# A slot's entry in DRAM widened from 4 to 64 bytes, with the lists read two jobs ahead, in a router of an attention and mixture-of-experts kernel

## The chip, the cores and the metric

The kernel runs on one core of one Trainium2 chip. The metric is the device time in microseconds (us); lower is better.

## The reference

Three stages follow each other; all data are float32 at the edges.

```python
# 1. linear attention with decay: batch 4, heads 8, sequence 768, head size 48
for t in range(S):
    cur = einsum('bhd,bhe->bhde', u[None] * kt, vt)
    y[:, :, t] = einsum('bhd,bhde->bhe', rt, state + cur)
    state = w[None, :, :, None] * state + einsum('bhd,bhe->bhde', kt, vt)
# 2. x has N = 3072 rows of D = 384; 8 experts, F = 1024; each row goes to one expert
logits = x @ w_gate
expert_idx = argmax(logits, axis=1)
for e in range(E):
    mask = expert_idx == e
    h = maximum(x[mask] @ w1[e], 0.0)
    out[mask] = gate_w[mask, None] * (h @ w2[e])
# 3. one dense layer for all rows, 384 -> 2048 -> 384, with an ELU between
h = x @ w_in
return where(h > 0, h, exp(minimum(h, 0)) - 1) @ w_out
```

## The kernel before, in words

**Attention and routing.** The sequence is cut into six chunks of 128 steps; a chunk has 4 x 128 tokens. While a chunk's attention runs on all engines, the chunk before it is routed. For each batch index of a chunk, `slots` works out where each of 128 tokens belongs: expert times 512 plus its rank among that expert's tokens so far, so that tokens of one expert get consecutive slots. `store` writes the tokens' rows to the DRAM array `xl` with one SP transfer for each chunk, and `place` writes, for each of the four batch indices, the token's row number into its slot of the DRAM array `xi`: one scatter (an indirect transfer issued by POOL, helper `scatter`, line 98) of 128 entries. There are 24 scatters. At the start `blank` fills `xi` and a second DRAM array, `idl`, with the number of an empty row (lines 274 and 275).

**The jobs.** The first expert layer runs as nine jobs (`JOBS`, called u = 0 to 8): two halves of the fullest expert, then the other seven experts by size. The order is worked out on the chip; SP and ScalarE read it into registers (`TENSOR_LOAD`). For each job, `load_i` has SP read the job's list of row numbers from `xi` (line 758; it must wait until all scatters so far have landed), `load_x` has POOL gather the rows from `xl` by that list (line 770; `xe` for jobs 0 to 2, `xg` later), `note` has SP write the list on to `idl` (line 783), `turn` transposes the rows on TensorE (line 798), and `layer1` and `layer2_columns` multiply (lines 829 and 869). Job 0 starts before routing is done, on the first four chunks' tokens, and overlaps the last chunk.

**Weights.** `Stream` reads weights in chunks of 768 KB through two buffers `raw` (line 695, on SP's queue) and splits each into a rounded half (ScalarE, line 705) and the rest (VectorE, line 711). Chunks 0 to 3 belong to jobs 0 and 1, chunks 4 to 7 to job 2, and so on. Each product is made of three matmuls, so both halves are needed. In job 0, activations are split the same way (ScalarE line 837, VectorE line 848).

**Order.** All steps up to the end of job 1's transposes are listed by `put(...)` and then called in the order of the table `ORDER`, written out by number; each engine runs its share in that order. The jobs from 1 on are a plain loop in `experts`, in which loads and splits are called between the matmuls.

**The second layer** goes through all 3,072 rows in six blocks of 512 (`layer2_rows`, line 1023). Its output rows are scattered to the output tensor (24 scatters of 128 rows, line 98 again) at positions that `tokens` works out from `idl`: the list is read as 24 rows of 128 (line 994), copied, transposed on TensorE (line 999) and turned into row numbers by a few small VectorE instructions.

Of the kernel before, what the change touches and what calls it, by code (L numbers as in the profile page):

```python
# [7 lines left out]
F32 = mybir.dt.float32  # L8
F32R = mybir.dt.float32r
BF16 = mybir.dt.bfloat16  # L10
I32 = mybir.dt.int32
# [4 lines left out]
PSUM = bass.MemoryType.PSUM  # L16

B, H, S, D = 4, 8, 768, 48
N, DM, E, F1, F2 = 3072, 384, 8, 1024, 2048
C = 128  # L20
NC_ = S // C
NP = H // 2
CAP = 512
HALF = CAP // 2
WIDTH = (480, 456, 424, 416, 408, 392, 384, 376)
JOBS = [(0, 0, HALF), (0, HALF, WIDTH[0] - HALF)] + [(p, 0, WIDTH[p]) for p in range(1, E)]
NJ = len(JOBS)
# [3 lines left out]
BLANK = N  # L31
# [34 lines left out]
)  # L66


# [35 lines left out]
def attention(tc, g, ctx, rkT, kv, wT, uT, wg):  # L104
    nc = tc.nc
# [123 lines left out]
    ef = con.tile([128, E], F32, name="ef")  # L229
    it = con.tile([128, ITEMS], I32, name="it")  # L230
    tid_i = con.tile([128, NC_, B], I32, name="tid_i")
    pos = con.tile([128, NC_, B], I32, name="pos")
    none = con.tile([128, (N + CAP) // 128], I32, name="none")
    zi = con.tile([128, E * CAP // 128], I32, name="zi")
    kr = con.tile([128, B, DM], F32, name="kr")
    acc, ones = g.acc, g.ones
    box = {}
# [15 lines left out]
    def iotas():  # L253
        nc.gpsimd.iota(ei, pattern=[[1, E]], base=0, channel_multiplier=0)
        nc.gpsimd.iota(it, pattern=[[1, ITEMS]], base=0, channel_multiplier=0)
        nc.gpsimd.tensor_copy(out=g.item, in_=it)
        for p in range(E):
            nc.gpsimd.memset(g.width[:, p:p + 1], float(WIDTH[p]))
        nc.gpsimd.iota(pos, pattern=[[B * C, NC_], [1, B]], base=0, channel_multiplier=B)
        nc.gpsimd.iota(tid_i, pattern=[[C, NC_], [S, B]], base=0, channel_multiplier=1)  # L260

    def router_constants():
# [3 lines left out]

    def blank():

        z = early_x.tile([128, 2, DM], F32, tag="xe", name="blank")[:, 0]
        nc.gpsimd.memset(z, 0.0)  # L270
        nc.gpsimd.memset(none, BLANK)
        nc.gpsimd.memset(zi, BLANK)
        nc.sync.dma_start(out=g.xl[BLANK:BLANK + 1], in_=z[0:1])
        nc.sync.dma_start(out=g.idl.rearrange("(p n) o -> p (n o)", p=128), in_=none)
        nc.sync.dma_start(out=g.xi.rearrange("(p n) o -> p (n o)", p=128), in_=zi)

    def krow(c, b):
        then(nc.vector.tensor_tensor(out=kr[:, b], in0=k_b[:, c % 2, b], in1=pkr.rearrange("s p h d -> s (p h d)"),
# [201 lines left out]
    def place(c):  # L480

        for b in range(B):
            scatter(tc, nc, g.apart, "slots", out=g.xi,
                    out_offset=bass.IndirectOffsetOnAxis(ap=r_t[c].si[:, b:b + 1], axis=0),
                    in_=pos[:, c, b:b + 1], in_offset=None, bounds_check=CAP * E - 1, oob_is_err=False)

    def counts():

# [101 lines left out]
    jobs.x_tile = lambda u, shape: (early_x if u < 2 else jobs.keep).tile(  # L590
        shape, F32, tag="xe", name="xe")
    jobs.xT_tile = lambda u, shape: (wk if u == 0 else jobs.keep).tile(shape, F32R, tag="kr", name="xTe", bufs=1)
    jobs.ix_tile = lambda shape: jobs.keep.tile(shape, I32, tag="ix", name="ix", bufs=NJ)
    jobs.h_tile = lambda f, shape: wk.tile(shape, F32R, tag="rp", name="he", bufs=4)

    def first_rows():
# [4 lines left out]
        put(jobs.note, 0)  # L601

    def next_rows():
        for u in range(1, NJ):
            put(jobs.load_i, u)
        for u in (1, 2):
            put(jobs.load_x, u)
        put(jobs.note, 1)
# [115 lines left out]
class Jobs:  # L724
# [27 lines left out]
    def load_i(self, u):  # L752

        p, at, n = JOBS[u]
        j = 2 if n <= HALF else 4
        ix = self.ix[u] = self.ix_tile([n // j, j])
        src = self.g.xi.rearrange("(e s) o -> e s o", e=E)[self.g.stream.which(p), at:at + n]
        self.nc.sync.dma_start(out=ix.unsqueeze(2), in_=src.rearrange("e (p j) o -> p (e j) o", j=j))

    def behind(self, ins):  # L760

# [1 line left out]

    def load_x(self, u, chunks=NC_):
        ix = self.ix[u]
        r, j = ix.shape
        x = self.x[u] = self.x_tile(u, [r, j, DM])
        rows = B * C * chunks if chunks < NC_ else BLANK + 1
        for i in range(j):
            ins = self.nc.gpsimd.indirect_dma_start(  # L770
                out=x[:, i, :], out_offset=None, in_=self.g.xl[0:rows],
                in_offset=bass.IndirectOffsetOnAxis(ap=ix[:, i:i + 1], axis=0), bounds_check=rows - 1,
                oob_is_err=False)
            if u > 2:
                self.behind(ins)

    def note(self, u):

        nc, g, (p, at, n) = self.nc, self.g, JOBS[u]
        if p > 0:  # L780
            at = nc.sync.value_load(g.lead[0:1, p:p + 1], min_val=0, max_val=sum(WIDTH[0:p]))
        ix = self.ix[u]
        nc.sync.dma_start(out=g.idl[bass.ds(at, n)].rearrange("(p j) o -> p j o", j=ix.shape[1]),
                          in_=ix.unsqueeze(2))

    def turn(self, u, k):
        self.turn_mm(u, k)
# [96 lines left out]
def experts(tc, g, ctx, wpk2, out):  # L884
# [77 lines left out]
    plan = overflow_plan(nc, g, own.enter_context(tc.tile_pool(name="m_p", bufs=1)), g.p_m)  # L962
    for u in range(1, NJ):
        for f in range(8):
            if 1 < u < NJ - 1 and f == 1:
                jobs.load_x(u + 1)
            stream.ahead(min(jobs.chunk(u, f) + 3, 4 * E + 4) if u > 1 else 4 + max(0, f // 2 - 1))
            if u + 1 < NJ and 5 <= f:
                jobs.turn(u + 1, f - 5)
                if f == 7:  # L970
                    jobs.note(u + 1)
            if f < 4 or u == 2:
                next(clearing, None)
            next(plan, None)
            for _ in range(1 + (f % 4 < 3 if u > 1 else f in (2, 4, 6))):
                next(narrowing, None)
            jobs.step(u, f)
# [7 lines left out]
    wq = own.enter_context(tc.tile_pool(name="n_w", bufs=4))  # L985
    ap = own.enter_context(tc.tile_pool(name="n_a", bufs=1, space=PSUM))
    lp = own.enter_context(tc.tile_pool(name="n_l", bufs=3, space=PSUM))
    tp_ps = own.enter_context(tc.tile_pool(name="n_t", bufs=1, space=PSUM))
    stream.pool = lambda i: wq if i >= 4 * E + 4 else stream.wc
    jobs.l_tile = lambda n: lp.tile([128, n], F32, tag="l", name="psl")  # L990
    t = jobs.keep.tile([128, 256 + 5 * N // 128], F32, tag="xe", name="idT")
    idi, idT = t[0:N // 128, 0:128].bitcast(I32), t[0:N // 128, 128:256]
    ids = t[:, 256:].bitcast(I32).rearrange("q (k n) -> q k n", k=5)
    nc.sync.dma_start(out=idi, in_=g.idl[0:N].rearrange("(n p) o -> n (p o)", p=128))

    def tokens():

        ps = tp_ps.tile([128, N // 128], F32, name="psi")
        nc.tensor.transpose(ps, idT, g.ident[0:N // 128, 0:N // 128])
        at, row, chunk, seq, none = (ids[:, k] for k in range(5))  # L1000
        nc.vector.tensor_copy(out=row, in_=ps)
        nc.vector.tensor_scalar(out=chunk, in0=row, scalar1=9, scalar2=7, op0=ALU.logical_shift_right,
                                op1=ALU.logical_shift_left)
        nc.vector.tensor_scalar(out=at, in0=row, scalar1=2, scalar2=127, op0=ALU.logical_shift_right,
                                op1=ALU.bitwise_and)
        nc.vector.tensor_scalar(out=seq, in0=row, scalar1=3, scalar2=None, op0=ALU.bitwise_and)
        nc.vector.tensor_scalar(out=none, in0=row, scalar1=float(BLANK), scalar2=OOB, op0=ALU.is_ge, op1=ALU.mult)
        nc.vector.tensor_tensor(out=at, in0=at, in1=chunk, op=ALU.add)
        nc.vector.tensor_tensor(out=at, in0=at, in1=none, op=ALU.add)
        nc.vector.scalar_tensor_tensor(out=at, in0=seq, scalar=float(S), in1=at, op0=ALU.mult, op1=ALU.add)  # L1010
# [27 lines left out]
    for u in range(NJ, NJ + 6):  # L1038
        for f in range(16):
            if u == NJ:  # L1040
                stream.ahead(jobs.chunk(u, f) + 3)
            if u == NJ and f == 2:
                nc.vector.tensor_copy(out=idT, in_=idi)
            if u == NJ and f == 4:
                tokens()
            if u + 1 < NJ + 6 and f in (6, 8, 10):
                jobs.take(u + 1, f // 2 - 3)
            if u == NJ + 5 and f == 14:
                jobs.LAG = 3
            jobs.step(u, f)  # L1050
# [142 lines left out]
def tile_kernel(tc, rkT, kv, wT, uT, wg, wpk, wpk2, out):  # L1193
# [1 line left out]
    g = K()  # L1195
    g.tc = tc
    g.xl = tc.dram_tile([BLANK + 1, DM], F32, name="xl")
    g.xi = tc.dram_tile([E * CAP, 1], I32, name="xi")
    g.idl = tc.dram_tile([N + CAP, 1], I32, name="idl")
    g.w2f = wpk2 if wpk2.dtype == F32 else tc.dram_tile([1, 8, 128, 1536], F32, name="w2f")  # L1200
    with ExitStack() as ctx:
        pool = ctx.enter_context(tc.tile_pool(name="const", bufs=1))
# [83 lines left out]
```

## Time and profile before

| | |
|---|---|
| Median of 3 runs | 819.2 us (818.52 to 819.9) |
| The profiled execution | 810.9 us, of which 809.1 us are the span from the first to the last instruction |
| Granted TensorE clock, mean over the span | 0.975 |
| TensorE busy (matmuls) | 769.8 us, 95% |
| VectorE / ScalarE / POOL busy | 486.2 / 346.8 / 132.8 us |
| Data moved by DMA | 84.92 MB in 24,660 packets, 8,620 of them under 512 bytes |

The profile is of one execution; every duration below is of that one. Times in the timeline count from the span's start. A row of the timeline has its start, its duration, the engine, the line, what is written and read, and in brackets how long the engine had been idle before it and what ended that. PE is TensorE's matmuls, PEld its weight loads, DVE VectorE, ACT ScalarE, POOL GpSimd, SPq the issue of transfers by SyncE. "DMA to landing" is the time from a transfer's issue until its semaphore showed that it had arrived. The DMA share is the mean busy share of the core's 16 DMA engines. A granted clock of 1.00 is 2.4 GHz, 0.50 is 1.2 GHz.

### The profile page before, as it was taken

What the parts mean: (1) busy time and instruction counts of PE and PEld (TensorE: products, weight loads), DVE (VectorE), ACT (ScalarE), POOL (GpSimd) and SP (SyncE); (2) the same over time, 40 slices, a digit from 0 to 9 for tenths busy, and PEclk for the clock granted to TensorE, in tenths of its full rate; (3) what the DMA queues carried; (4) which work ended last, traced back from release to release, by engine and by line L of the source; (5) the groups of instructions that cost most, each with busy time, mean ns of one, the idle gap of its engine ahead of it and who ended that gap; (6) DMA issues with size and microseconds to landing.
All of it is one profiled execution on the core that took longest, in us unless ns stands there. A gap on an engine that the chain in (4) does not pass through costs nothing. (4 is left out here: it accounts for less than half of the span.)

```text
span 809.1 us, 13146 instructions
## 1 busy us (share of the span) xinstructions
PE 769.8 (95%) x5113; PEld 690.6 (85%) x5114; DVE 486.2 (60%) x905; ACT 346.8 (43%) x675; POOL 132.8 (16%) x191
## 2 busy tenths in 40 slices
PE   6798799849999999999999999999999999999996
PEld 4576677649999999999989999999999999999996
DVE  6895975525987888866577444444444534544443
ACT  3686676426644444444444333233333333333231
POOL 4343442512320221030000020020002002002002
PEclk9699899979999999999999999999999999999999
DMA  9889434956978777865231010010001001001001
GB/s 341 201 177 150 120 80 80 158 76 183 308 212 275 253 266 230 258 168 163 92 118 40 1 40 0 2 40 1 0 1 40 1 1 40 1 1 40 1 0 42
DMA packets 24660, 84.92 MB, mean 105 GB/s; under 512 B 8620, under 2 KB 9013, under 8 KB 24017
## 3 DMA queue, kind: packets, MB, share of 16 engines
q1 hardware_dynamic: 17776, 74.01, 33.7%
q0 software_dynamic: 6528, 9.89, 4.0%
q8 instruction: 42, 0.69, 0.4%
q14 instruction: 26, 0.20, 0.1%
q10 hardware_dynamic: 288, 0.13, 0.1%
HBM read 68.20 MB, written 15.79 MB: 104 GB/s over the span
## 5 line engine op out<-in xcount | busy, mean ns | idle before, releaser
L829 PE MATMUL psl<-xT,wc 128*128 128x512 f32 (+7 forms) x1368 | 319.7, 378 | 0.1
L829 PEld LDWEIGHTS psl<-xT,wc 128*128 128x128 f32 x1368 | 251.6, 188 | 31.9 <-DVE xT L815 0.9
L1023 PE MATMUL acc<-wc,h 128*128 128x384 f32 x1152 | 217.8, 337 | 0.1
L1023 PEld LDWEIGHTS acc<-wc,h 128*128 128x128 f32 x1152 | 204.6, 188 | 8.7 <-DVE h L851 0.4
L841 DVE TENSOR_SCALAR ex<-ex 128x512 f32<-128x512 f32 x96 | 40.9, 426 | 125.1 <-ACT ex L840 125.1
L840 ACT ACTIVATE ex<-psl 128x512 f32<-128x512 f32 x96 | 57.3, 597 | 134.9 <-PE psl L829 134.9
L843 ACT CAST h<-ex 128x512 fp32r<-128x512 f32 x96 | 59.6, 621 | 126.1 <-DVE ex L842 126.1
L869 PE MATMUL acc<-h,wc 128*128 128x224 f32 (+7 forms) x576 | 111.8, 339 | 0.0
L851 DVE TENSOR_TENSOR h<-ex,h 128x512 fp32r<-128x512 f32 x96 | 66.5, 692 | 65.9 <-ACT h L843 65.9
L711 DVE TENSOR_TENSOR wc<-raw,wc 128x768 fp32r<-128x768 f32 x80 | 73.1, 955 | 52.4 <-ACT wc L705 52.4
L869 PEld LDWEIGHTS acc<-h,wc 128*128 128x128 f32 x576 | 100.8, 188 | 1.9
L98 POOL DMA_INDIRECT out_dram<-y,idT x24 | 24.6, 1024 | 424.4 <-ACT y L1031 418.9
L705 ACT CAST wc<-raw 128x1536 fp32r<-128x1536 f32 x40 | 59.1, 1477 | 39.9 <-PE acc L869 27.2
L842 DVE TENSOR_TENSOR ex<-ex,psl 128x512 f32<-128x512 f32 x96 | 66.0, 688 | 3.3
L333 ACT ACTIVATE a<-ident,cs 128x128 f32<-128x128 f32 x192 | 59.1, 392 | 1.3 <-issue 1.2
L837 ACT ACTIVATE h<-psl 128x224 fp32r<-128x224 f32 (+7 forms) x64 | 31.5, 492 | 58.6 <-PE psl L829 56.0
L770 POOL DMA_INDIRECT xg<-xl,ix x24 | 34.5, 1437 | 131.5 <-PE psl L829 126.0
L349 DVE COPY_PREDICATED a<-above,psc 128x512 f32<-128x512 uint32 x48 | 33.3, 729 | 12.6 <-PE psc L341 10.6
L848 DVE SCALAR_TENSOR_TENSOR h<-psl,h 128x224 fp32r<-128x224 f32 (+7 forms) x64 | 35.3, 551 | 8.2 <-ACT h L837 8.2
L369 PE MATMUL pso<-a,v 128*48 128x128 f32 x384 | 28.1, 289 | 6.7 <-DVE a L349 6.2
L218 POOL TENSOR_TENSOR rt<-rkb,ex 128x512 f32<-128x512 f32 x20 | 24.0, 1208 | 61.7 <-DVE a L349 21.3
L341 PE MATMUL psc<-rt,kt 64*128 64x128 f32 x384 | 30.8, 300 | 1.6 <-DVE a L349 1.6
(179 smaller groups left out, 611.1 us busy)
## 6 DMA issues: line engine op xcount, KB each, us to landing
raw<-in_wpk_dram SPq DMA_DIRECT2D x32, 768.0 KB, 6.6
r<-in_wpk_dram SPq DMA_DIRECT2D x16, 768.0 KB, 5.8
w2f<-f SPq DMA_DIRECT2D x16, 384.0 KB, 5.3
raw<-w2f SPq DMA_DIRECT2D x8, 768.0 KB, 4.2
v<-in_kv_dram SPq DMA_DIRECT2D x6, 768.0 KB, 4.2
rkb<-in_rkT_dram SPq DMA_DIRECT2D x12, 384.0 KB, 7.6
xl<-x SPq DMA_DIRECT2D x6, 768.0 KB
kb<-in_kv_dram SPq DMA_DIRECT2D x5, 768.0 KB, 6.1
```

Source lines behind the costliest of these rows:

```text
L333: nc.scalar.activation(out=a[:, b, :], in_=g.ident, func=ACTF.Copy, scale=cs_t[c][:, b, p, hf:hf + 1])
L705: self.nc.scalar.copy(out=w[:, 0], in_=self.loaded[i])
L711: self.nc.vector.tensor_tensor(out=w[:, 1, at], in0=r[:, at], in1=w[:, 0, at].bitcast(F32), op=ALU.subtract)
L829: self.mm = nc.tensor.matmul(ps, self.w1(i, a, k, fi), xT[:, b, k], start=(m == 0), stop=(m == 8))
L840: nc.scalar.activation(out=ex, in_=ps, func=ACTF.Exp)
L841: nc.vector.tensor_scalar(out=ex, in0=ex, scalar1=1.0, scalar2=-1.0, op0=ALU.min, op1=ALU.add)
L842: nc.vector.tensor_tensor(out=ex, in0=ex, in1=ps, op=ALU.max)
L843: nc.scalar.copy(out=h[:, 0], in_=ex)
L848: nc.vector.scalar_tensor_tensor(out=h[:, 1], in0=ps, scalar=0.0, in1=h[:, 0].bitcast(F32), op0=ALU.max, op1=ALU.subtract)
L851: nc.vector.tensor_tensor(out=h[:, 1], in0=self.ex, in1=h[:, 0].bitcast(F32), op=ALU.subtract)
L869: nc.tensor.matmul(self.acc[u][k], w[:, a, 128 * k:128 * k + 128], h[:, b], start=(f == 0 and m == 0), stop=(f == 7 and m == 2))
L1023: nc.tensor.matmul(acc, h[:, a, 128 * j:128 * j + 128], jobs.w2(i, b, fi), start=(f == 0 and m == 0), stop=(f == 15 and m == 2))
```

## The change

Every entry of `xi` and of `idl` becomes a row of `COPIES` = 16 equal 32-bit numbers, 64 bytes. The scatters write 16 numbers for each token (`pos` holds each row number 16 times); the lists are read and noted whole, and the gathers take the first of each 16. `blank` fills the wider arrays from one tile, with a source row that is used twice. Of the later jobs' lists, which were all read in one go after the last scatter, only those of jobs 1 and 2 are read there; the loop over the jobs reads the list of job u + 2 at the beginning of job u, and five list buffers take turns where each job had its own. In the second layer the list is read straight into 128 partitions, so the copies and the transpose go, and the VectorE instructions come four steps later. `ORDER` is renumbered for the list reads that left it.

```diff
+COPIES = 16
...
-    pos = con.tile([128, NC_, B], I32, name="pos")
-    none = con.tile([128, (N + CAP) // 128], I32, name="none")
-    zi = con.tile([128, E * CAP // 128], I32, name="zi")
+    pos = con.tile([128, NC_, B, COPIES], I32, name="pos")
...
-        nc.gpsimd.iota(pos, pattern=[[B * C, NC_], [1, B]], base=0, channel_multiplier=B)
+        nc.gpsimd.iota(pos, pattern=[[B * C, NC_], [1, B], [0, COPIES]], base=0, channel_multiplier=B)
...
-        z = early_x.tile([128, 2, DM], F32, tag="xe", name="blank")[:, 0]
+        z = early_x.tile([128, 2, DM], F32, tag="xe", name="blank")
+        z, none = z[:, 0], z[:, 1].bitcast(I32)
         nc.gpsimd.memset(z, 0.0)
         nc.gpsimd.memset(none, BLANK)
-        nc.gpsimd.memset(zi, BLANK)
         nc.sync.dma_start(out=g.xl[BLANK:BLANK + 1], in_=z[0:1])
-        nc.sync.dma_start(out=g.idl.rearrange("(p n) o -> p (n o)", p=128), in_=none)
-        nc.sync.dma_start(out=g.xi.rearrange("(p n) o -> p (n o)", p=128), in_=zi)
+        for t in (g.idl, g.xi):
+            n = t.shape[0] // 256 * COPIES
+            nc.sync.dma_start(out=t.rearrange("(p k n) o -> p k (n o)", p=128, k=2),
+                              in_=none[:, 0:n].unsqueeze(1).to_broadcast([128, 2, n]))
...
-                    in_=pos[:, c, b:b + 1], in_offset=None, bounds_check=CAP * E - 1, oob_is_err=False)
+                    in_=pos[:, c, b], in_offset=None, bounds_check=CAP * E - 1, oob_is_err=False)
...
-    jobs.ix_tile = lambda shape: jobs.keep.tile(shape, I32, tag="ix", name="ix", bufs=NJ)
+    jobs.ix_tile = lambda shape: jobs.keep.tile(shape, I32, tag="ix", name="ix", bufs=5)
...
-        for u in range(1, NJ):
+        for u in (1, 2):
             put(jobs.load_i, u)
...
-        ix = self.ix[u] = self.ix_tile([n // j, j])
+        ix = self.ix[u] = self.ix_tile([n // j, j, COPIES])
...
-                in_offset=bass.IndirectOffsetOnAxis(ap=ix[:, i:i + 1], axis=0), bounds_check=rows - 1,
+                in_offset=bass.IndirectOffsetOnAxis(ap=ix[:, i, 0:1], axis=0), bounds_check=rows - 1,
...
     for u in range(1, NJ):
         for f in range(8):
+            if u + 2 < NJ and f == 0:
+                jobs.load_i(u + 2)
...
-    idi, idT = t[0:N // 128, 0:128].bitcast(I32), t[0:N // 128, 128:256]
-    nc.sync.dma_start(out=idi, in_=g.idl[0:N].rearrange("(n p) o -> n (p o)", p=128))
+    rows = t[:, 0:COPIES * N // 128].rearrange("q (n o) -> q n o", o=COPIES)
+    nc.sync.dma_start(out=rows, in_=g.idl[0:N].rearrange("(n p) o -> p n o", p=128))
...
-        ps = tp_ps.tile([128, N // 128], F32, name="psi")
-        nc.tensor.transpose(ps, idT, g.ident[0:N // 128, 0:N // 128])
-        nc.vector.tensor_copy(out=row, in_=ps)
+        row = rows[:, :, 0]
...
-            if u == NJ and f == 2:
-                nc.vector.tensor_copy(out=idT, in_=idi)
-            if u == NJ and f == 4:
+            if u == NJ and f == 8:
                 tokens()
...
-    g.xi = tc.dram_tile([E * CAP, 1], I32, name="xi")
-    g.idl = tc.dram_tile([N + CAP, 1], I32, name="idl")
+    g.xi = tc.dram_tile([E * CAP, COPIES], I32, name="xi")
+    g.idl = tc.dram_tile([N + CAP, COPIES], I32, name="idl")
```

On SP, where weight chunk 3 has been issued and the lists of the later jobs are read, this stood before (partitions x elements behind each transfer; 104x4 is job 4's list, 112x2 job 1's, 96x4 job 7's):

```order
L695 DMA raw<-in_wpk_dram 128x1536
L688 TENSOR_LOAD order
L688 ISA x2
L758 ISA
L758 DMA ix<-xi 104x4
L758 ISA
L758 DMA ix<-xi 112x2
L688 TENSOR_LOAD order
L688 ISA x2
L758 ISA
L758 DMA ix<-xi 96x4
```

and this stands there now (112x32 is job 1's list, 114x64 job 2's, 106x64 job 3's; the other lines' numbers are two higher than before):

```order
L697 DMA raw<-in_wpk_dram 128x1536
L760 ISA
L760 DMA ix<-xi 112x32
L690 TENSOR_LOAD order
L690 ISA x2
L760 ISA
L760 DMA ix<-xi 114x64
L785 DMA idl<-ix 112x32
L690 TENSOR_LOAD order
L690 ISA x2
L760 ISA
L760 DMA ix<-xi 106x64
```

Before, five more lists, job 2's the sixth of the eight behind job 4's and job 1's, and then job 1's note stood ahead of the load of chunk 4; now that load comes right behind job 3's list, and job 1's note stands ahead of job 3's list.

At SP's start, the fills of the two arrays stand between the loads of k, v and r rows. Before:

```order
L143 DMA kb<-in_kv_dram 128x1536
L273 DMA xl<-blank 1x384
L274 DMA idl<-none 128x28
L275 DMA xi<-zi 128x32
L147 DMA v<-in_kv_dram 128x1536
```

Now:

```order
L145 DMA kb<-in_kv_dram 128x1536
L273 DMA xl<-blank 1x384
L276 DMA idl<-blank 256x1x224
L276 DMA xi<-blank 256x1x256
L149 DMA v<-in_kv_dram 128x1536
```

Nothing moved there; the two fills grew sixteenfold, in the same place of the queue.

## Rows read from the trace of the kernel before

**Rows 1.** The page's 40 slices: TensorE's busy tenths; GB/s moved by DMA

```profile
PE   6798799849999999999999999999999999999996
...
GB/s 341 201 177 150 120 80 80 158 76 183 308 212 275 253 266 230 258 168 163 92 118 40 1 40 0 2 40 1 0 1 40 1 1 40 1 1 40 1 0 42
```

**Rows 2.** Waits of PE: who waited for whom, us in total, times, longest

```profile
PE psl L829 <- DVE he L848: 11.0, 1, 11.0
PE pso L369 <- DVE a L349: 6.2, 1, 6.2
...
PE psq L798 <- DMA xe<-xl,ix: 0.9, 2, 0.5
```

**Rows 3.** Timeline, PE and ACT, 156 to 184 us

```profile
156.91 3.83 PE L829 MATMUL psl<-xTe,wc 128*128 128x256 f32 x27
...
168.68 1.47 ACT L705 CAST wc<-raw 128x1536 fp32r<-128x1536 f32 x1 [11.23 <-DMA raw<-in_wpk_dram]
...
172.82 2.26 PE L829 MATMUL psl<-xTe,wc 128*128 128x256 f32 x9 [11.02 <-DVE he L848]
...
183.43 0.55 PE L798 MATMUL psq<-ident,xe 112*128 112x112 f32 x4
```

**Rows 4.** Timeline, issues on SP, 141 to 182 us

```profile
141.10 0.34 SPq L783 DMA_DIRECT2D idl<-ix  x1
...
149.00 0.34 SPq L695 DMA_DIRECT2D raw<-in_wpk_dram  x1
...
172.56 8.60 SPq L758 DMA_DIRECT2D ix<-xi  x8
```

**Rows 5.** DMA issues of the whole span: count, KB each, median us to landing

```profile
raw<-in_wpk_dram SPq DMA_DIRECT2D x32, 768.0 KB, 6.6
...
rkb<-in_rkT_dram SPq DMA_DIRECT2D x12, 384.0 KB, 7.6
...
idl<-none SPq DMA_DIRECT2D x1, 14.0 KB
xi<-zi SPq DMA_DIRECT2D x1, 16.0 KB
```

**Rows 6.** Timeline, the hole in attention, 66 to 87 us

```profile
66.63 0.78 SPq L137 DMA_DIRECT2D rkb<-in_rkT_dram  x2
...
80.92 1.29 DVE L223 TENSOR_TENSOR rp<-rkb 128x512 f32<-128x512 f32 x2 [8.88 <-DMA rkb<-in_rkT_dram]
...
85.03 1.94 PE L369 MATMUL pso<-a,v 128*48 128x128 f32 x14 [6.22 <-DVE a L349]
```

**Rows 7.** Tile xi, 57 to 66 us: landing of the first batch of scatters

```profile
DMA to landing us min/median/max: 8.0/9.6/11.2
```

**Rows 8.** Tile xi, 152 to 160 us: the last batch of scatters and its landing

```profile
L98 POOL DMA_INDIRECT xi<-pos,si x4: 971/974/1521, 153.0 to 157.3; - x4
...
DMA to landing us min/median/max: 15.2/15.3/15.5
```

**Rows 9.** Tile out_dram: landing of the output's scatters

```profile
DMA to landing us min/median/max: 2.6/2.6/4.4
```

**Rows 10.** Windows: length, busy PE, PEld, DVE, ACT, POOL, clock, DMA share, GB/s

```profile
8.00:14.00 6.00, 2.61 (x64) 2.20 (x64) 4.57 (x9) 1.02 (x3) 2.52 (x20) 0.96 1.03 415
73.00:76.00 3.00, 3.00 (x43) 1.95 (x35) 0.00 (x0) 0.75 (x2) 0.00 (x0) 1.00 0.85 38
141.00:145.00 4.00, 3.53 (x57) 2.89 (x54) 3.79 (x14) 0.86 (x2) 2.23 (x3) 1.00 0.68 29
164.00:167.00 3.00, 0.00 (x0) 0.00 (x0) 0.00 (x0) 0.00 (x0) 0.00 (x0) 1.00 0.74 68
172.00:177.20 5.20, 4.38 (x20) 4.41 (x21) 1.74 (x6) 1.74 (x2) 0.41 (x1) 0.50 0.14 39
```

**Rows 11.** Timeline, DVE at 21 us, in the start

```profile
20.75 0.69 DVE L213 TENSOR_TENSOR kt<-rkb,er 128x512 f32<-128x512 f32 x1 [1.58 <-DMA rkb<-in_rkT_dram]
```

**Rows 12.** Timeline, POOL: the second gather of job 1's rows

```profile
178.13 1.46 POOL L770 DMA_INDIRECT xe<-xl,ix  x1 [0.30 <-issue]
```

More of the change, by code (lines that the diff above doesn't have):

```diff
@@ L755, in load_i @@
         j = 2 if n <= HALF else 4
-        ix = self.ix[u] = self.ix_tile([n // j, j])
+        ix = self.ix[u] = self.ix_tile([n // j, j, COPIES])
         src = self.g.xi.rearrange("(e s) o -> e s o", e=E)[self.g.stream.which(p), at:at + n]
-        self.nc.sync.dma_start(out=ix.unsqueeze(2), in_=src.rearrange("e (p j) o -> p (e j) o", j=j))
+        self.nc.sync.dma_start(out=ix, in_=src.rearrange("e (p j) o -> p (e j) o", j=j))
     def behind(self, ins):
@@ L765, in load_x @@
         ix = self.ix[u]
-        r, j = ix.shape
+        r, j = ix.shape[0:2]
         x = self.x[u] = self.x_tile(u, [r, j, DM])
@@ L783, in note @@
         nc.sync.dma_start(out=g.idl[bass.ds(at, n)].rearrange("(p j) o -> p j o", j=ix.shape[1]),
-                          in_=ix.unsqueeze(2))
+                          in_=ix)
     def turn(self, u, k):
@@ L987, in experts @@
     lp = own.enter_context(tc.tile_pool(name="n_l", bufs=3, space=PSUM))
-    tp_ps = own.enter_context(tc.tile_pool(name="n_t", bufs=1, space=PSUM))
     stream.pool = lambda i: wq if i >= 4 * E + 4 else stream.wc
     jobs.l_tile = lambda n: lp.tile([128, n], F32, tag="l", name="psl")
-    t = jobs.keep.tile([128, 256 + 5 * N // 128], F32, tag="xe", name="idT")
-    idi, idT = t[0:N // 128, 0:128].bitcast(I32), t[0:N // 128, 128:256]
-    ids = t[:, 256:].bitcast(I32).rearrange("q (k n) -> q k n", k=5)
-    nc.sync.dma_start(out=idi, in_=g.idl[0:N].rearrange("(n p) o -> n (p o)", p=128))
+    t = jobs.keep.tile([128, (COPIES + 4) * N // 128], I32, tag="xe", name="ids")
+    rows = t[:, 0:COPIES * N // 128].rearrange("q (n o) -> q n o", o=COPIES)
+    ids = t[:, COPIES * N // 128:].rearrange("q (k n) -> q k n", k=4)
+    nc.sync.dma_start(out=rows, in_=g.idl[0:N].rearrange("(n p) o -> p n o", p=128))
     def tokens():
-        ps = tp_ps.tile([128, N // 128], F32, name="psi")
-        nc.tensor.transpose(ps, idT, g.ident[0:N // 128, 0:N // 128])
-        at, row, chunk, seq, none = (ids[:, k] for k in range(5))
-        nc.vector.tensor_copy(out=row, in_=ps)
+        row = rows[:, :, 0]
+        at, chunk, seq, none = (ids[:, k] for k in range(4))
         nc.vector.tensor_scalar(out=chunk, in0=row, scalar1=9, scalar2=7, op0=ALU.logical_shift_right,
```

8 rows, old and new, of the table ORDER are left out of this document.

## Prediction

> **What bounds the kernel now.** I read five views in this order. First the page's slices [rows 1]: TensorE is busy 9 tenths or more in nearly every slice from the tenth on, so from some 180 us to the end the kernel runs at TensorE's pace, and a later start of that part moves the end by as much. The holes lie before it. Then what TensorE waited for [rows 2]: two single waits stand out, 11.0 us (the first layer of job 0, on VectorE's half of its activations) and 6.2 us (attention's output, on the masked scores). Neither ends at VectorE; the timeline leads on.
>
> The 11.0 us [rows 3, 4]: TensorE stops at 172.82 - 11.02 = 161.80. VectorE's activation stands behind its half of the split of weight chunk 2, that behind ScalarE's half (line 705), and ScalarE had waited 11.23 us for the transfer of that chunk. SP issued it at 149.00 and it was there at 168.68: 19.7 us, where such a load mostly takes 6.6 us [rows 5].
>
> The 6.2 us [rows 6]: VectorE waits 8.88 us for the r and k rows whose load SP issued at 66.63; they come at 80.92, after 14.3 us, where 7.6 us is usual for a load of that size [rows 5].
>
> What holds up two loads that were issued early? Both follow a batch of four slot scatters, which land 8.0 to 11.2 us after their start in the first batch and 15.2 to 15.5 us in the last [rows 7, 8]; the scatters of 1,536-byte rows into the output, the same instruction from the same queue, take 2.6 us [rows 9]. And the windows [rows 10]: at the start the DMA engines are full and move 415 GB/s; just after the slot scatters they are 0.85 and 0.74 busy and move 38 and 68 GB/s. They stand, they don't carry. The same happens from 141 to 145 (0.68 busy, 29 GB/s), where until its very end no scatter runs but SP has just written job 0's list, at 141.10 [rows 4], in pieces of 8 bytes. So I take it that the writes of 4 and 8 bytes to DRAM hold the engines, whichever queue they come from. Whether it is the size, or that many writers share a neighbourhood (tokens of one expert take consecutive slots, so some sixteen entries of a scatter lie side by side), no row tells.
>
> **The change part by part.**
>
> *Scatters of 64 bytes.* Still 24 instructions with 128 rows each; only each row's length grows. No row shows a 64-byte scatter. The bounds are the 4-byte ones (15.3 us in the last batch) and the 1,536-byte ones (2.6 us). I take a value near 2.6, since the row shows that width, not the instruction or its count, is what differs between the two, and since entries of one scatter no longer lie within 64 bytes of each other.
>
> *First hole.* With 7.6 us the r and k rows come at 74.2 instead of 80.92. VectorE needs 85.03 - 80.92 = 4.1 us from there to the masks that TensorE waits for, so they are ready at 78.3, before TensorE gets there (85.03 - 6.22 = 78.8). All **6.2 us** go, with 0.5 us to spare; if the load still took 10 us, 4.3 would go.
>
> *Rows of job 0.* Their list and gather follow the same small writes; TensorE waits 0.9 us for them [rows 2]. I count **0.9 us**, between 0 and 0.9.
>
> *Second hole.* With 6.6 us chunk 2 is there at 155.6, before ScalarE asks for it (168.68 - 11.23 = 157.4). ScalarE's split (1.47 us) and what followed took from 168.68 to 172.82, 4.1 us, so TensorE could go on at 157.4 + 4.1 = 161.6, just before it stops. All **11.0 us** go; a load of 10 us would leave 1.6 of them. Chunk 3 comes behind it on the same queue and is wanted only for the last quarter of the layer. After the hole TensorE ran at a granted clock of 0.50, its level of 1.2 GHz, to 177.2 [rows 10]: nine first-layer matmuls took 2.26 us, where three such groups take 3.83 us before the hole, 1.28 each [rows 3]. Of the 4.38 us that TensorE is busy there 4.38 x 1.28 / 2.26 = 2.5 would be left at the full level: **1.9 us** more (the same after the first hole I leave to the range).
>
> *What is late next.* TensorE's next wait is for job 1's rows. Its list can be read only when the last scatter has landed. Before, the lists began at 172.56 and TensorE transposed the rows at 183.43, 10.9 us later, of which some 0.5 us was job 4's list, now behind. The last scatter starts at 157.3 [rows 8]; landing after 3.8 us (somewhat over 2.6, since chunk 3 is in flight) the rows are there at 157.3 + 3.8 + 10.4 = 171.5. TensorE wants them at 183.43 - 11.02 - 1.9 = 170.5, so **-1.0 us** is given back: between 0 and, if the scatter lands after 8.0 us, -5.2.
>
> *The fills.* They grow from 14 and 16 KB [rows 5] to 224 and 256 KB, in a stretch in which the engines are full and VectorE waits for r and k rows behind them (1.58 us, [rows 11]). 450 KB at 415 GB/s are **-1.1 us**; at the 201 GB/s of the page's second slice [rows 1] -2.3; at the least 0, if the wait had slack elsewhere.
>
> *The lists.* SP read eight lists in one go before chunk 4's load; now three, and job 1's note waits for job 1's list to land, with job 3's list and chunk 4's load queued behind it. Chunk 4 is used from job 2 on, after all of job 1, and its split waits for a weight buffer that job 1 still reads, so this costs nothing; without that cover it would be one list's latency. The later lists and notes (256 bytes a row) and the second layer's list (3,072 pieces of 64 bytes, between two weight loads that are read three chunks ahead) lie beside TensorE's work: nothing. One small transpose and two VectorE copies go: nothing that counts.
>
> The sum: 6.2 + 0.9 + 11.0 + 1.9 - 1.0 - 1.1 = 17.9 us. The profiled execution took 810.9 us (span 809.1), which gives 793.0; the median of the runs is 819.2, 8.3 us above that execution, and no row says where these lie, so I take the gain from the median: **801.3 us**.
>
> **The rivals.**
> 1. *Half.* The stall goes with the number of small writes, and 64 bytes only soften it: loads still late by a third to a half, or job 1's rows come 5 us late and the second hole moves there. For it: 24 scatters stay. Against it: the width is all that separates the scatters of [rows 8] and [rows 9]. Half of the 19.0 us that the stalls give, less the fills' 1.1 and some of the late rows, is 7 to 9: about 811.
> 2. *None.* A row of 64 bytes is still far below 1,536 and is treated like one of 4: both holes stay and the fills cost their 1.1 us, 820.3. Against it speak the fills of 112 and 128 bytes a partition, issued at about 9 us, beside which the engines still move 415 GB/s [rows 10]. The page "DMA: Bandwidth & Descriptors" (Specifications) of the Trainium skill gives this rule: transfers under 512 bytes are done as read-modify-write; by it 64 bytes gain nothing. The rows can't refute it for 64 bytes. The same would come out if the row were split into sixteen pieces, so that the change doesn't do what it says; the destination is now 4,096 rows of 16, one row for each index.
> 3. *Slower.* What holds the engines is the number of separate places that a scatter touches: some eight stretches now, 128 after it. It decides if the scatters land later than 15.3 us. With landing twice as long, the two loads come another 9.6 and 15.3 us later (medians of [rows 7, 8]): 819.2 + 24.9 + 1.1 = 845. For it: the 1,536-byte scatters run with no other load beside them, so 2.6 us is a quiet figure. Against it: the gathers, 128 separate rows each, pass within 5.3 us [rows 3, 12].
>
> **How the numbers follow.** The sum's case has 0.72, half 0.13, none 0.08, slower 0.07. A measurement here can tell about 0.2%, 1.6 us, from no change; none's 1.1 us is within it. So faster 0.85, same 0.08, slower 0.07. The bounds of the terms: at best 6.2 + 0.9 + 11.0 + 1.9 plus some 3 us of clock after the first hole and before the second, and nothing given back, 23; with a little of the unexplained 8.3 us, 793. At worst 4.3 + 0 + 9.4 + 1 - 5.2 - 2.3 = 7.2, 812; half ends there too. The range is 793 to 812.
>
> **What would show it.** Right: scatters landing within 5 us in every batch; no wait of ScalarE for chunk 2 over 1 us; VectorE's wait before line 223 at about 74 us under 3; windows after the scatters in which share and GB/s go together; VectorE's waits before 21 us longer by 1.1. A scatter still holds POOL about 1 us. Wrong: landings over 8 us, POOL's time in a scatter grown, or the 11 us hole moved to the transposes of job 1.

## The result, and the profile after

The changed kernel took **805.8 us** (median of 4 runs, 799.2 to 807.7) beside 819.1 us for the kernel before on the same chip (818.5 to 819.9): a ratio of 0.985, 95% interval 0.982 to 0.988, 13.4 us less. Forecast were 801.3 us, 793 to 812. The profiled execution after took 805.7 us (span 803.9). That of before, 810.9 us, was a lucky one, 8.2 us under the median of its kernel, so the two profiles differ by only 5.2 us.

The changed kernel's page and the waits of PE; the latter stand against [rows 2]:

```profile
PE   5799999879999999999999999999999999999997
...
GB/s 317 224 181 187 112 82 109 194 136 166 258 244 214 265 267 266 239 179 147 112 95 40 1 40 0 2 40 1 1 0 40 1 1 40 1 1 40 1 0 42
...
PE psg L293 <- DVE kr L280: 6.0, 3, 4.2
PE psq L800 <- DMA xe<-xl,ix: 5.8, 2, 3.8
```

The 11.0 and the 6.2 us are gone from the list. What leads it now was short before: the start (line 293, behind VectorE's products of the first loads) and job 1's rows (line 800). Its timelines of ACT, DVE, POOL, SP and PE, which answer to [rows 3, 4, 6, 11, 12]:

```profile
156.32 1.47 ACT L707 CAST wc<-raw 128x1536 fp32r<-128x1536 f32 x1
162.44 1.47 ACT L707 CAST wc<-raw 128x1536 fp32r<-128x1536 f32 x1
...
18.82 0.69 DVE L225 TENSOR_TENSOR rp<-rkb 128x512 f32<-128x512 f32 x1 [2.58 <-DMA rkb<-in_rkT_dram]
...
71.18 2.53 DVE L225 TENSOR_TENSOR rp<-rkb 128x512 f32<-128x512 f32 x4
...
165.20 1.47 POOL L772 DMA_INDIRECT xe<-xl,ix  x1 [7.38 <-PE psl L831]
166.97 0.99 POOL L772 DMA_INDIRECT xe<-xl,ix  x1 [0.30 <-issue]
...
161.22 1.49 SPq L760 DMA_DIRECT2D ix<-xi  x2
...
166.20 1.02 SPq L697 DMA_DIRECT2D raw<-in_wpk_dram  x2
...
171.65 0.32 PE L800 MATMUL psq<-ident,xe 112*128 112x112 f32 x1 [1.96 <-DMA xe<-xl,ix]
175.77 0.82 PE L800 MATMUL psq<-ident,xe 112*128 112x112 f32 x3 [3.81 <-DMA xe<-xl,ix]
```

ScalarE starts the splits of chunks 2 and 3 with no wait, and VectorE's products at 71.18 find their rows there. (A bracket is the idle time before an instruction and what ended it.) But at 18.82 VectorE waits 2.58 us for r and k rows, and PE stands 1.96 and 3.81 us for job 1's two gathers, issued at 165.20 and 166.97; two weight loads leave SP in the same stretch. The windows, with columns as in [rows 10]:

```profile
64.00:68.00 4.00, 3.16 (x53) 2.47 (x51) 2.42 (x5) 2.59 (x10) 2.76 (x6) 1.00 0.99 172
72.00:76.00 4.00, 4.00 (x48) 2.59 (x44) 3.70 (x6) 3.93 (x14) 1.30 (x1) 1.00 0.97 188
172.00:176.00 4.00, 0.23 (x1) 0.23 (x2) 0.00 (x0) 0.00 (x0) 1.67 (x2) 0.55 0.91 221
176.00:180.00 4.00, 4.00 (x24) 4.00 (x23) 0.76 (x2) 0.69 (x2) 0.00 (x0) 0.59 0.09 31
```

Behind the first batches of scatters the engines now carry 172 and 188 GB/s where they stood at 38. That is not quite what the same share carried just before the first scatter (0.98 busy with 236 GB/s from 54 to 58 us). The last two rows show the price of the new hole: the granted clock falls to 0.55 in it and is 0.59 in the 4 us behind it.

### The profile page after: what moved, and what is told of

Read it like the earlier page. It is cut to its first block, busy times and chain, and to the rows that moved or that the text cites. A ratio compares the mean times of both kernels' runs of the same rounds, so it can differ in the third digit from the quotient of the medians.

```text
span 803.9 us, 13146 instructions
## 1 busy us (share of the span) xinstructions
PE 772.6 (96%) x5113; PEld 691.0 (86%) x5113; DVE 485.2 (60%) x903; ACT 347.3 (43%) x675; POOL 131.0 (16%) x190
## 5 line engine op out<-in xcount | busy, mean ns | idle before, releaser
L100 POOL DMA_INDIRECT out_dram<-y,ids x24 | 24.6, 1026 | 423.8 <-ACT y L1032 417.9
L343 PEld LDWEIGHTS psc<-rt,kt 64*128 64x128 f32 x384 | 25.4, 193 | 8.4 <-issue 5.5
```

The lines of the kernel that those rows point to most:

```text
L343: nc.tensor.matmul(ps[hf][:, b, :], kt[r0:r0 + 64, b, :], rt[r0:r0 + 64, b, :], start=True, stop=True, skip_group_check=True)
```

## The experiments

The 12 runs fall into three groups, each timed beside the kernel before: medians 814.6 (e1 to e4), 820.9 (f1 to f4) and 820.7 us (g1 to g4). So ratios are compared across groups and times only within one.

**1. Is it the width?** The changed kernel with narrow entries:

```
-COPIES = 16
+COPIES = 1
```

> The changed kernel with entries of 4 bytes again; the lists read two jobs ahead and the second layer's list without a transpose stay. If the entries' width removed the stalls (my theory): both holes come back, chunk 2 lands about 19 us after its issue, packets of xi after a batch again take several us, the time is about 817 (814 to 822). If the order of the lists did it: no hole before L223 or L831, about 806. If half came from each: about 812.

Measured: 820.4 us, ratio 1.007 (1.004 to 1.010). Waits of PE, ACT's timeline, and the median landing of the scatters:

```profile
PE psl L831 <- DVE he L850: 7.1, 1, 7.1
PE pso L371 <- DVE a L351: 5.6, 1, 5.6
...
167.18 1.47 ACT L707 CAST wc<-raw 128x1536 fp32r<-128x1536 f32 x1 [7.25 <-DMA raw<-in_wpk_dram]
180.17 1.47 ACT L707 CAST wc<-raw 128x1536 fp32r<-128x1536 f32 x1 [6.17 <-DMA raw<-in_wpk_dram]
...
xi<-pos,si POOLq DMA_INDIRECT x24, 10.5
```

Both holes are back, and ScalarE waits for chunk 2 and then for chunk 3. The width alone is worth 0.985 / 1.007 = 0.978, about 18 us; the other parts (lists two jobs ahead, no transpose) gain nothing and with 4-byte entries cost some 0.7%. Part of that may be job 1's rows, for which PE waits 3.2 us in this trace, and the start, where TensorE is already 1.7 us later than before at 66 us; no run was made for either alone.

**2. What about a small write costs: its size, or its neighbours?** The slots stay 64 bytes apart, but a scatter writes 4 bytes of one:

```
+        nc.vector.tensor_scalar(out=r.si, in0=slot, scalar1=float(COPIES), ...
-            scatter(tc, nc, g.apart, "slots", out=g.xi,
+            scatter(tc, nc, g.apart, "slots", out=g.xi.rearrange("a (o u) -> (a o) u", u=1),
-                    in_=pos[:, c, b], ...
+                    in_=pos[:, c, b, 0:1], ...
```

> Entries stay 64 bytes apart in DRAM, but a slot scatter writes only the first 4 bytes of one. Theory A, a small write costs by its own size: the stalls of the slot scatters are back (share near 1 with under 70 GB/s behind a batch), the first hole is back and in part the second; about 815 (811 to 821). Theory B, what costs is that 4-byte writes share 64-byte neighbourhoods: no stalls, scatters land in under 5 us, the time is that of the changed kernel, about 806 (801 to 808). The one added DVE operation per batch (0.16 us, 6 times) is under 1 us in both.

Measured: 797.3 us, ratio 0.980 (0.977 to 0.982). PE's longest wait, what is left of the attention hole and of the wait for job 1's rows, and the median landing of the scatters:

```profile
PE psg L293 <- DVE kr L280: 6.1, 3, 4.4
...
PE pso L371 <- DVE a L351: 0.6, 1, 0.6
...
PE psq L801 <- DMA xe<-xl,ix: 0.3, 1, 0.3
...
xi<-pos,si POOLq DMA_INDIRECT x24, 3.6
```

Both holes stay away: 0.6 us is left of the one in attention, and no wait of job 0's first layer is in the list. So a write of 4 bytes isn't slow by its size; what hurts is that many land close together. How close? The same with the fills moved (part 4), 64, 16 and 32 bytes apart:

```
-COPIES = 16
+COPIES = 4     (f2; 8 in g2; f1 keeps 16)
```

> Both edits together: slot scatters of 4 bytes into entries 64 bytes apart (e2_apart was 0.9795 of the kernel before) and the fills at 44 us (e4_fill_late was 0.9762; the changed kernel 0.9847). If the two gains are of different stretches and add: 0.971. If the apart kernel was only spared the wait for job 1's rows by chance: 0.976 as e4_fill_late, with 4 us or more of waits ahead of job 1's transposes.

> As f1_apart_late with entries of 16 bytes, so that four entries of different tokens lie in each 64 bytes; a slot scatter still writes 4 bytes, and the fills are a quarter. If entries disturb each other only inside 16 bytes or less: the time of f1_apart_late or up to 2 us less (0.968 to 0.971). If they do so inside 32 or 64 bytes: the stalls are back, scatters land in 8 us and more, 0.985 to 0.995.

> As f1_apart_late and f2_apart16_late with entries 32 bytes apart. 64 bytes apart gave 0.9774 with scatters landing fast, 16 bytes apart 0.9944 with a median landing of 7.0 us. If the neighbourhood in which small writes disturb each other is over 32 bytes: between them, about 0.985, landing 5 us or more. If it is 32 bytes or less: 0.970 to 0.977 and a landing of about 3.5 us, with half of the fills.

Measured: 64 bytes apart 0.977 (0.972 to 0.983), 16 bytes 0.994 (0.992 to 0.997), 32 bytes 0.986 (0.982 to 0.990). For 16 bytes the waits of PE, two windows behind slot scatters, and the landing of the scatters (three of the 24 show one, here and at 32 bytes):

```profile
PE psq L801 <- DMA xe<-xl,ix: 6.5, 2, 5.3
PE pso L371 <- DVE a L351: 3.4, 1, 3.4
...
68.00:72.00 4.00, 4.00 (x38) 2.39 (x40) 4.00 (x6) 3.97 (x14) 1.28 (x1) 1.00 1.19 103
152.00:156.00 4.00, 2.02 (x14) 1.20 (x14) 3.61 (x19) 3.55 (x7) 0.20 (x1) 0.92 1.39 131
...
DMA to landing us min/median/max: 6.7/7.0/8.3
```

The same windows and the landing for 32 bytes:

```profile
68.00:72.00 4.00, 4.00 (x48) 2.53 (x42) 4.00 (x7) 3.97 (x15) 0.86 (x2) 1.00 0.69 129
152.00:156.00 4.00, 4.00 (x29) 3.85 (x28) 2.21 (x12) 2.57 (x4) 3.14 (x6) 0.83 0.61 201
...
DMA to landing us min/median/max: 2.5/4.1/5.1
```

At 16 bytes the engines are again busy throughout and carry little (1.19 for 103 GB/s, 1.39 for 131), and the attention hole is half back. At 32 bytes share and GB/s go together (0.69 for 129, 0.61 for 201), and TensorE keeps within about 1.6 us of the 64-byte version until 350 us. So the trace shows the disturbance at 16 bytes and none at 32. The 32-byte version's time doesn't fully follow: it is between the two, its interval touches that of 64 bytes, and what costs it some 0.9% was not found (2.9 us of it, in its profile, is one wait for a late gather that ends at 355 us, and that other kernels show in some executions too). Wider spacing also stretches the whole array, from 16 to 256 KB, and leaves fewer entries in any larger block; whether the distance itself decides, or that, no run separates.

**3. Do the jobs' notes do the same, from SP's queue?** Slots wide, the second layer's list narrow; in f4 a note writes single 4-byte entries (its expectation took them for 8 or 16 bytes), in g1 2 or 4 at a time as before:

```
-    g.idl = tc.dram_tile([N + CAP, COPIES], I32, name="idl")
+    g.idl = tc.dram_tile([N + CAP, 1], I32, name="idl")
-                          in_=ix)
+                          in_=ix[:, :, 0:1])
```

and in g1, in place of the last line,

```
+        few = self.keep.tile(list(ix.shape[0:2]), I32, tag="few", name="few", bufs=2)
+        nc.gpsimd.tensor_copy(out=few, in_=ix[:, :, 0])
...
+                          in_=few.unsqueeze(2))
```

> The changed kernel with the second layer's list at 4 bytes an entry again (the jobs' notes write 8 or 16 bytes at a time), slots at 64 bytes. If the jobs' notes had a share in the stall behind job 0's note: chunk 1 and chunk 2 land 4 us later than in the changed kernel, ratio 0.988 to 0.993. If only the slot scatters stalled the engines: 0.983 to 0.985, a little less than the changed kernel since the fill shrinks by 210 KB.

> Slots at 64 bytes as in the changed kernel; the jobs' notes as in the kernel before: 4 bytes an entry in DRAM, written 2 or 4 entries at a time (8 or 16 bytes; f4_slots_only wrote them one by one and was 27 us over the changed kernel). A small POOL copy per job (about 0.2 us, POOL idle there) gathers the entries. If the notes of before did harm: 3 to 10 us over the changed kernel of the same call, job 0's rows or chunk 1 late, and waits of the weight stream behind later jobs' notes. If only single 4-byte writes do: within 1 us of the changed kernel, or up to 2 us less since a fill shrinks.

Measured: f4 835.4 us, ratio 1.018 (1.013 to 1.024), far over both theories. Its waits of PE, a note on SP, and two windows around it:

```profile
PE acc L871 <- DVE h L850: 12.8, 8, 2.7
...
198.20 0.99 SPq L785 DMA_DIRECT2D idl<-ix  x1
...
196.00:200.00 4.00, 4.00 (x39) 4.00 (x38) 3.39 (x9) 2.71 (x4) 0.00 (x0) 1.00 0.80 284
208.00:212.00 4.00, 4.00 (x21) 3.64 (x20) 0.65 (x2) 0.00 (x0) 2.73 (x2) 1.00 0.91 57
...
213.69 1.48 ACT L707 CAST wc<-raw 128x1536 fp32r<-128x1536 f32 x1 [6.29 <-DMA raw<-in_wpk_dram]
```

SP's plain DMA now does to the engines what POOL's scatters did (0.91 busy, 57 GB/s), ScalarE waits 6.29 us for the weight load behind it, and it happens in job after job (13 such waits, 49.9 us). In g1 the time is 810.2 us, ratio 0.983 (0.977 to 0.989), beside 805.4 us, 0.981 (0.978 to 0.984) for the changed kernel of the same group: no difference that the intervals allow. The stall is there all the same. Windows of g1, then of the changed kernel (g3), behind job 0's note (136.56 and 135.87) and chunk 1's load (137.11 and 136.42):

```profile
137.00:139.00 2.00, 2.00 (x28) 1.62 (x26) 1.05 (x5) 1.79 (x2) 1.41 (x2) 1.00 1.41 50
142.00:144.00 2.00, 2.00 (x32) 1.64 (x29) 1.83 (x11) 0.30 (x1) 0.00 (x0) 1.00 0.96 391
```

```profile
137.00:139.00 2.00, 2.00 (x34) 1.71 (x35) 1.83 (x8) 1.46 (x2) 1.69 (x2) 1.00 0.81 215
139.00:141.00 2.00, 1.53 (x28) 1.25 (x28) 2.00 (x4) 0.58 (x1) 0.14 (x1) 1.00 0.94 375
```

With pieces of 8 bytes the engines are first busy at 50 GB/s, and the chunk moves at 142 to 144 us, with 128-byte rows at 137 to 141: some 4 us later, but nobody waits for chunk 1 then.

**4. What do the fills cost?** Their work item, moved in the table that sets the order, so that SP issues them at 45.88 and 46.59 in place of 8.84 and 9.54:

```
-    0, 5, 4, 22, 1, 6, 8, 23, 31, 27, 24, ...
+    0, 5, 4, 22, 1, 6, 8, 23, 31, 24, ...
-    ... 120, 146, 106, 68, ...
+    ... 120, 146, 27, 106, 68, ...
```

> The changed kernel, with the three fills of DRAM put behind the second batch of loads in SP's queue (about 44 us in place of 8.5). If the wide fills cost the 2.5 to 5.5 us by which the changed kernel's PE is late at 20 to 70 us: about 802 (3 to 5 us less). If the lateness there has another cause (the clock, the loads themselves): 805 to 807. If the fills hurt as much at 44 us: 805 to 808.

Measured: 796.2 us, ratio 0.976 (0.972 to 0.980). That lies below the changed kernel's 0.982 to 0.988, but touches the 0.978 to 0.984 that the same kernel gave in part 6. At the start the gain is plain: PE's longest wait is 2.1 instead of 4.2 us, and VectorE's product that waited 2.58 us finds its rows there:

```profile
16.27 0.69 DVE L225 TENSOR_TENSOR rp<-rkb 128x512 f32<-128x512 f32 x1
...
PE psq L800 <- DMA xe<-xl,ix: 6.1, 1, 6.1
PE psg L293 <- DVE kr L280: 3.9, 3, 2.1
```

Against e3 of the same group (802.3 us, which otherwise is the changed kernel but for job 2's gathers) e4 takes 6.1 us less. The fills did not give that. From the starts of the same instructions in both traces, TensorE is 2.3 us earlier at 66 us but 0.5 at 104, and some 5 us come only where e3 waits for a later job's rows:

```profile
353.29 0.30 PE L800 MATMUL psq<-ident,xg 94*128 94x94 f32 x1 [3.57 <-DMA xg<-xl,ix]
```

Against the two traces of the changed kernel e4 is 3.9 and 4.4 us ahead at 66 us, and 3.6 and 2.5 at 104. So the late fills are worth some 2 to 4 us at the start, and 0.5 to 3.6 once attention has waited elsewhere. Not all of that is the bytes': two loads that stood behind the fills now leave SP at 3.85 and 4.50 us instead of 10.19 and 10.85.

**5. Why are job 1's rows late?** e3 issues job 2's gathers only once job 1's first layer runs; f3 holds weight chunk 4 (and 5 behind it) as well, and has the late fills:

```
-            put(jobs.load_x, u)                          (u = 2 leaves the early list)
+            if u < NJ - 1 and f == 1: jobs.load_x(u + 1)
+            if u > 1: self.behind(ins)
f3 also:
+            if u > 1 or f > 0: stream.ahead(...)
+        if i == 4: self.g.jobs.behind(ins)
```

> The changed kernel, but job 2's four gathers are issued only once job 1's first layer has begun, so they don't run beside job 1's gathers. If the new 5.8 us of waits ahead of job 1's transposes come from bandwidth shared with these gathers: the second gather lands 2 to 4 us earlier, about 803 (2 to 4 us less than the changed kernel's 805.8). If they come from the two weight chunks issued at 166.2 or from latency alone: no change, 805 to 807.

> The changed kernel with the fills at 44 us, and both job 2's gathers and weight chunks 4 and 5 held until job 1's first layer has begun. If these chunks' 1.5 MB, issued within 2 us of job 1's gathers, made job 1's rows late: under 2 us of waits ahead of job 1's transposes in place of 6.1 (e4_fill_late), ratio 0.970. If the gathers are late by themselves (latency of list, then rows): still 4 us and more, 0.975 to 0.978.

Measured: e3 802.3 us, ratio 0.985 (0.982 to 0.988), as the change; f3 0.980 (0.974 to 0.985). Waits of PE in e3, then in f3 (`xe` are the rows of jobs 0 and 1, `xg` in these two those of later jobs):

```profile
PE psq L800 <- DMA xg<-xl,ix: 6.1, 4, 3.6
...
PE psq L800 <- DMA xe<-xl,ix: 4.3, 2, 2.2
```

```profile
PE psq L802 <- DMA xg<-xl,ix: 6.5, 4, 2.8
```

With job 2's gathers held, 4.3 of 5.8 us of waits for job 1's rows are left; with the weight chunks held as well, none. That points to the chunks' 1.5 MB more than to the gathers; no run holds the chunks alone. What was held is then late itself, the rows of jobs 2 and on, so in these two runs the wait only moved. The loads beside them are not enough to make the rows late: in e2 nothing was held, SP issued the chunks from 159.02 on, just ahead of the second gather at 159.35, and its rows were there 5.3 us later (0.3 us of wait). In f1, with the same slots, PE waits 5.6 us. Why is open, and so whether 4 bytes beat a whole 64-byte entry.

**6. Once more, both kernels.**

> The changed kernel once more, beside the others: 0.985 of the kernel before. If the 3.3 us that its profile lost at 104 to 126 us belong to that one execution: not there again, or elsewhere. If they belong to the change: there again.

> The kernel before, looked at a second time, since its profiled execution was 8.3 us under its median. If executions differ by chance in small steps of the tensor engine: its two holes are there at 5 to 12 us each, and what differs lies spread over 0 to 200 us. If one stall differs: one gap is longer by most of the 8 us.

Measured: the changed kernel 805.4 us, ratio 0.981 (0.978 to 0.984); a single further execution of the kernel before 820.2 us. Waits of PE in that execution, against [rows 2]:

```profile
PE psg L291 <- DMA v<-in_kv_dram: 4.6, 2, 2.9
PE psl L829 <- DVE he L848: 4.0, 1, 4.0
PE pso L369 <- DVE a L349: 3.9, 1, 3.9
PE psg L291 <- DVE kr L278: 3.8, 2, 2.1
PE psl L829 <- ACT wc L705: 2.5, 1, 2.5
```

The 11 us hole isn't there. The same stalls are paid in other places: 2.9 + 3.9 us in attention, 4.0 for chunk 2, 2.5 for chunk 3, and TensorE falls back a little in every batch between. The losses of the changed kernel at 104 to 126 us (3.3 us against its profile partner) came again in g3, and like ones in g4, but in none of e2 to e4; they go with the group of runs, not with the change, and their cause is open.

## Why the prediction was right, and where it was not

How much later (+) or earlier (-) TensorE runs with the change, taken from the starts of the same TensorE instruction in both traces. The second pair (g4, g3) is of one group and of ordinary executions of both kernels:

| up to | first pair, us | second pair, us | forecast of the step |
|---|---|---|---|
| 37 to 66 us: the start, the fills | +4.9 | +3.4 | +1.1 |
| 90 us: first hole | -8.5 | -9.6 | -6.2 |
| 158 us: batches between, job 0's rows | +3.0 | -5.8 | -0.9 |
| 176 (190) us: second hole and clock | -12.9 | -9.2 | -12.9 |
| 185 (193) us: job 1's rows | +7.2 | +4.5 | +1.0 |
| the end | -5.0 | -16.0 | -17.9 |

(The rest, +1.3 in the first pair and +0.7 in the second, lies behind these rows.)

**Cause: right.** Narrow entries bring the stalls back, SP's notes make them too, and neighbourhood, which the text left open beside size, decides. Of the two reasons given for a short landing, the width of a row is not the one that holds (in e2, 4 bytes land in 3.6 us); the spacing, that entries no longer lie within 64 bytes of each other, is. The page "DMA: Bandwidth & Descriptors" (Specifications) of the Trainium skill has transfers under 512 bytes done as read-modify-write; that 64 bytes would then gain nothing is not borne out here, where entries of 64 bytes (0.985), and 4 bytes written 64 apart (0.980), are free of the holes. Nearer is the page "Collectives: The Full Stack" (Rules for kernel authors) of the Trainium skill: for collectives it wants buffers aligned to 32 bytes to prevent read-modify-write, and 16 against 32 bytes is where f2 and g2 part. That a read-modify-write is what holds the engines no run shows.

**First and second hole: right in cause, and in size for the second**, -8.5 (forecast -6.2) and -12.9 in the pair on which the sum was made, the 1.9 us of clock within the latter. But the step "the sum is taken from the median" stood on one execution's holes, and an ordinary execution of before has other ones. That the totals agree (17.9 and 16.0) is in part luck: 5.8 us came from the batches between, which the sum didn't count.

**Fills: the term was mis-sized.** 1.1 us, bounded by 2.3; measured 3.4 to 4.9 us of late TensorE by 66 us. The 450 KB were priced at the engines' rate. Shown: the wait behind them grew to 2.58 us from these rows of before, PE's behind it from 2.4 to 4.2, and e4 has both back.

```profile
16.34 0.69 DVE L223 TENSOR_TENSOR rp<-rkb 128x512 f32<-128x512 f32 x1 [1.06 <-DMA rkb<-in_rkT_dram]
...
PE psg L291 <- DVE kr L278: 4.2, 3, 2.4
```

The rate was about right (391 GB/s from 8 to 14 us), but the bytes are not all of it: in e1, whose fills are again 14 and 16 KB, TensorE is already 1.7 us late at 66 us, so that part came with what e1 shares with the change (the fills are written as 256 pieces each, for one). No run separates it.

**Job 1's rows, and the lists: here a step failed.** 1.0 us with 5.2 as its bound; measured 4.5, and 7.2 in the first pair, the clock within. The landing of the last scatters fits: the list went out at 161.22, forecast 161.1. Wrong was "the rows are there" 10.4 us after that; they were there 14.6 us after it (175.77). The step took the gathers' time over from before and costed the shorter queue of lists at nothing. Before, SP's eight lists took 8.60 us [rows 4] and so kept chunks 4 and 5 behind the gathers (POOL issued the second gather at 178.13, [rows 12], and SP the chunks as here):

```profile
181.85 0.98 SPq L695 DMA_DIRECT2D raw<-in_wpk_dram  x2
```

With three lists the two chunks go out from 166.20 on, and the gathers of 165.20 and 166.97 need 6.4 and 8.8 us, where the second needed 5.3. The forecast asked when chunk 4 is wanted, not what its load would be in the way of. f3, with them held, has no such wait; that they alone make it is not shown, since in e2 they stood there too and the rows were in time.

**Notes, second layer's list, transpose: nothing**, as forecast; no wait in the traces names them.

**The signs to look for.** No wait for chunk 2, no wait before line 225, POOL at 0.97 us a scatter: seen. Share and GB/s go together far better than before, though not fully (0.97 for 188). The changed kernel's trace shows no landing of a scatter; in e4 and e2 the median is 3.2 and 3.6 us over all batches, but "within 5 us in every batch" was too tight: in the first, with loads beside it, it is 7.9 and 6.7, and one in e4 took 8.5, over the 8 us that were to speak against the forecast. "VectorE's waits longer by 1.1" was 1.5. And of the sign of being wrong, the hole moved to job 1's transposes, about half is there: 5.8 us of waits.

**The rivals.** Half: its time (811) is about as far from the result as the forecast is. Loads late by a third to a half are not there, except at 16 bytes; its other branch, job 1's rows 5 us late with part of the second hole moved there, is. None: refuted. Slower, by separate places: refuted by e2, whose scatters touch the same 128 places each.

## What to carry to other kernels

Small writes to DRAM that fall side by side can hold up the DMA engines for microseconds, from POOL's queue and from SP's; spread 64 bytes apart they made no such hole here, even where each still wrote only 4 bytes (32 bytes apart the trace is clean too, but the time lies between). Look for windows in which the engines are busy and carry little, and then at what was written just before. A big cheap transfer (a fill) still belongs where nothing urgent queues behind it, and what a removed stall sets free will all be fetched at once: ask what the next wait shares its bandwidth with. When two runs differ, look where in the trace they part before the edit gets the credit: of the 6.1 us between e3 and e4, some 5 come only at about 355 us.

## What was not expected of the hardware

- A write of 4 bytes costs a scatter no more than one of 64 when it has its neighbourhood for itself: median landings 3.6 and 3.2 us (e2, e4), against 10.5 us side by side (e1).
- Single 4-byte writes from SP's own queue are as harmful: 57 GB/s at a share of 0.91, and some 27 us in all (f4 against the change: 1.018 against 0.985, of 820 us).
- The same program loses the same stalls in other places from one execution to the next: a hole of 11.0 us in one profile, and none over 4.0 in another that took 9.3 us longer.
